# Channel words in half chunks, a fixed order for the last expert slots, and VectorE's part in the first mixing batch

## The chip, the cores and the metric

The kernel runs on one core of a Trainium2 chip. The metric is the device time of one execution in microseconds (us). The engines are TensorE (PE in the profile, with PEld for its weight loads), VectorE (DVE), ScalarE (ACT), GpSimd (POOL) and SyncE (SP, which issues nearly all DMAs).

## What is computed

Three stages follow each other: attention, a mixture of experts, and a mixing layer. The first two only set the stage here; of the third the reference says, for x of shape (4, 576, 512):

```
theta = x @ w_theta
zr, zi = x * cos(theta), x * sin(theta)
y = einsum('ts,bsd->btd', w_tok_r, zr) + einsum('ts,bsd->btd', w_tok_i, zi)
u = x + y
out = u + maximum(u @ w_ch, 0)
```

The experts give each token `p[e] * (relu(x @ w1[e]) @ w2[e])` for the one expert e that its gate chooses. The weights of the mixing layer come as 64-bit floating-point numbers.

## The kernel before

Products are made from high and low parts: an operand is rounded to fp32r by a ScalarE copy (the high part), a subtraction gives what is left (the low part), and three matmuls stand for one. So a weight or an activation needs a copy on ScalarE and a subtraction on VectorE or GpSimd before TensorE can take it.

**Experts.** Tokens are sorted by expert into slots: three early single slots, one late single slot, eight slots of two blocks of 128 tokens, and two final single slots, 14 in all, numbered by `i` in `run_slots`. `two_step` does a slot of two blocks, `single_step` one of 128 tokens. A step loads the next slot's weights (`load_w1`, `load_w2`), splits them (`split_w1`, `split_w2`, L1097 and L1098), gathers and transposes its tokens (`tokens`, L939), runs the hidden layer (`hidden`, L1024 to L1030), and finishes the slot before (`finish_slot`, L1063 to L1067). The finished rows are scaled on ScalarE (L1080) and scattered to memory by GpSimd (L1086). The scaled rows of a slot of two blocks and the relu of a single slot (L1037) share one buffer, `h`. The steps `i` up to `n + 1` also finish what is left over.

**Decoding.** The 64-bit mixing weights are read as pairs of 32-bit words and turned into fp32 on the way, in the idle time of the slots. `stage_words` asks for a chunk (L1153), and `decode_chunk` is a generator of four VectorE steps (L1189, L1193, L1196, L1198), with a square on GpSimd (L1190); `split_last` then gives the high part on ScalarE (L1179) and the low part on GpSimd (L1180). `decode(k)` advances it by k steps. The channel weights `w_ch` are the last, from slot `CHANNEL_AT` = 11 on: four chunks of 512 columns, with one buffer for words and one for values.

**Order.** PE, ACT and DVE follow the order of the program inside a `manual_schedule` block; SP and POOL are ordered by the scheduler of the compiler. Each slot is a block of its own, and the instructions of neighbouring blocks can be put among each other.

**Mixing.** Tokens are handled in four batches, each in two halves of 256 columns (`dh`). `theta` makes the angle in three groups of token chunks (two of 512 columns, the third of 256), `wave_steps` turns a group into zr and zi in steps, each `yield` ending one: range reduction on VectorE (L1398 to L1404), sine and cosine on ScalarE (L1405 to L1407), products with x on VectorE (L1410, L1412, L1419), then the high parts on ScalarE (L1426) and the low parts on GpSimd (L1427). `wave("0011")` advances groups 0, 0, 1, 1 by one step each. `mix` adds up 27 matmuls in the order of `MIX_ORDER` (L1440 to L1442), `mix_out` adds x (L1453) and, behind every second mix, splits the sum (L1455, L1456). There are two buffers for the result of a mix. `channel` is the last product, `store` the output. The calls in `mix_all` are the order of PE, ACT and DVE.

Of the kernel before, what the change touches and what calls it, by code (L numbers as in the profile page):

```python
# [10 lines left out]
F32 = mybir.dt.float32  # L11
# [3 lines left out]
AF = mybir.ActivationFunctionType  # L15
# [6 lines left out]
DM = H * D  # L22
# [13 lines left out]
WARM = 10  # L36
RING, HIDDEN_STEPS, LAST_STEPS = 3, 4, 5
MANUAL = {mybir.EngineType.PE, mybir.EngineType.Activation, mybir.EngineType.DVE}
# [14 lines left out]
class Kernel:  # L53
    def __init__(self, ctx, tc, ins, out, scratch):
        self.ctx, self.tc, self.nc = ctx, tc, tc.nc
        self.ins, self.out = ins, out
        self.scratch = scratch
        self.dec = iter(())

# [3 lines left out]
    def constants(self):  # L63
# [11 lines left out]
        scr = cp.tile([P, 256], I32, name="scr_i")  # L75
        self.w8 = cp.tile([P, E], F32, name="w8")
        nc.gpsimd.iota(scr[:, 0:E], pattern=[[-1, E]], base=E, channel_multiplier=0)
        nc.gpsimd.tensor_copy(self.w8, scr[:, 0:E])
        self.ebase = cp.tile([P, E], F32, name="ebase")
        nc.gpsimd.iota(scr[:, 8:8 + E], pattern=[[NT, E]], base=0, channel_multiplier=0)  # L80
# [698 lines left out]
    def run_slots(self, state, first=True):  # L779
# [10 lines left out]
        for i in range(0 if first else -1, n + 2):  # L790
            if first and i == OPEN_AT:
                self.right.close()
                self.open_mix_weights()
            if first and i == CHANNEL_AT:
                self.open_channel_weights()
            with self.tc.manual_schedule(engines=MANUAL):
                self.slot_step(state, i, first)

    def slot_step(self, state, i, first=True):
# [20 lines left out]
    def two_step(self, now, nxt, last, old, after):  # L820
# [4 lines left out]
        for f in range(4):  # L825
# [13 lines left out]
            elif f < 3:  # L839
                self.split_w2(now, f)  # L840
            self.decode(STEPS[0])
        for c in range(3):
# [9 lines left out]
        for c in range(2, 4):  # L852
            self.split_w1(nxt, c)
        self.decode(STEPS[1])
        for h in range(2):
# [3 lines left out]
    def single_step(self, now, nxt, last, old, final, over, begin, after):  # L859
# [6 lines left out]
        if final:  # L866
            self.decode(HIDDEN_STEPS)
        if nxt:
            for c in range(2):
                self.load_w1(nxt, c)  # L870
                self.split_w1(nxt, c)
        if now:
            self.relu(now, 0)
        if nxt:
            for c in range(2, 4):
                self.load_w1(nxt, c)
                self.split_w1(nxt, c)
        if now:
            self.relu(now, 1)
# [224 lines left out]
    def open_mix_weights(self):  # L1104
# [13 lines left out]
        self.todo += [(self.wt[:, 0, i], self.wt[:, 1, i], rows[j]) for i, j in enumerate(MIX_ORDER)]  # L1118
        self.active, self.last, self.one_val = [], [], False
        self.dec = self.decoder()  # L1120
# [3 lines left out]
    def open_channel_weights(self):  # L1124
# [4 lines left out]
            [P, 2, 4, DM], F32R, name="ch")  # L1129
        self.open_stage(1, 1)  # L1130
        self.one_val = True
        self.todo = self.square_words("moe2_w_ch", self.ch)
        self.stage_words()

# [47 lines left out]
    def decode_chunk(self, h, l, w, last):  # L1182
        nc = self.nc
        lo, hi = w[:, :, 0], w[:, :, 1]
        if self.one_val:
            self.split_last(last)
        val = self.val.tile([P, h.shape[1]], F32, name="val")
# [11 lines left out]
        last.append((h, l, val))  # L1199
        self.stage_words()  # L1200
        yield 1
# [26 lines left out]
    def mix_all(self):  # L1228
# [16 lines left out]
        self.prep(0, (), (3, 4))  # L1245
        self.wave("0000" "21111" "00" "0" "2222" "11" "1" "22" "2")
        self.waves(0, 1)
        self.wave("012")
        self.rest = []
        for b in range(B):  # L1250
            more = b + 1 < B
            self.mix(b, 0, 0)
            while self.rest:
                self.rest.pop(0)()
            self.mix_out(b, 0, 0)
            self.wave("0011" "0" if b else "01010101")
            self.mix(b, 0, 1)
            self.mix_out(b, 0, 1)
            self.wave("1" if b else "2222" "0011" "01")
            self.mix(b, 0, 2)  # L1260
            self.mix_out(b, 0, 2)
            self.wave("222")
            self.mix(b, 0, 3)
            self.mix_out(b, 0, 3)
            if more:
                self.load_x(b + 1)
# [4 lines left out]
            self.mix(b, 1, 1)  # L1271
            self.mix_out(b, 1, 1)
            if more:
                chunks = (2, 3) if b % 2 == 0 else (2, 3, 4)
# [11 lines left out]
            self.mix(b, 1, 3)  # L1286
            self.mix_out(b, 1, 3)
            if more:
                self.theta(b + 1, 1, 0)
# [91 lines left out]
    def wave_steps(self, b, dh, g):  # L1381
# [39 lines left out]
        else:  # L1421
            r = x
        for z, n in ((k, "r"), (q, "i")) if g < 2 else ((r, "m"),):
            zh = self.zp.tile([P, w, HD], F32R, name=f"z{n}h{g}")
            zl = self.zp.tile([P, w, HD], F32R, name=f"z{n}l{g}")
            nc.scalar.activation(zh, z, AF.Copy)  # L1426
            nc.gpsimd.tensor_tensor(zl, z, zh.bitcast(F32), ALU.subtract)  # L1427
            for i, c in enumerate(cs):
                st["z", dh, 8 if n == "m" else c + 4 * (n == "i")] = zh[:, i], zl[:, i]

    def mix(self, b, dh, g):
# [12 lines left out]
    def mix_out(self, b, dh, g):  # L1444
# [8 lines left out]
        nc.vector.tensor_tensor(u[:, zs], st["y"], st["xf", dh][:, d, zs], ALU.add)  # L1453
        if z == 1:
            nc.scalar.activation(uu[:, 0], u, AF.Copy)  # L1455
            nc.vector.tensor_tensor(uu[:, 1], u, uu[:, 0].bitcast(F32), ALU.subtract)  # L1456

# [101 lines left out]
```

## Time and profile before

| | us |
|---|---|
| median of 3 runs | 854.56 (854.49 to 854.65) |
| the profiled execution | 854.62 |
| its span, first to last instruction | 852.8 |
| TensorE busy | 811.4 (95%) |
| VectorE busy | 609.9 (72%) |
| ScalarE busy | 493.9 (58%) |
| GpSimd busy | 210.9 (25%) |

The profile covers the span; 1.82 us of the execution's time lie outside it. A busy share is an average over stages with different limits. Experts end and mixing begins at about 604 us.

### The profile page before, as it was taken

Reading aid. Unit: us, or ns where it says so; the run is one execution under the profiler, and the core shown is the slowest. Engines: PE = TensorE matmul, PEld = TensorE weight load, DVE = VectorE, ACT = ScalarE, POOL = GpSimd, SP = SyncE. Lnnn points to the kernel's source line nnn. Section 1 sums busy time; section 2 is a strip of 40 time slices with the busy share of each in tenths; the row PEclk is TensorE's granted clock in tenths of the full one; section 3 lists DMA queues with packets and bytes.
Section 4 is the critical chain, followed back from the end, with each engine's and each line's share of the span. In section 5 each row is a group of like instructions: output and inputs, shape, how many; then the busy total and the mean of one; then the engine's idle time right before and its main releaser. Section 6 shows DMA issues by size and latency. Waiting matters only on the chain.

```text
span 852.8 us, 15168 instructions
## 1 busy us (share of the span) xinstructions
PE 811.4 (95%) x5554; PEld 651.8 (76%) x5554; DVE 609.9 (72%) x1281; ACT 493.9 (58%) x883; POOL 210.9 (25%) x209
## 2 busy tenths in 40 slices
PE   7999999999999987899999999997898999999997
PEld 5555556656566555578999889985788999999997
DVE  6888787888979848856878888777486635755422
ACT  5888776777776654655665555546554435435311
POOL 3000002002103014421645554532023320332120
PEclk9999999999999999899999999999999999999999
DMA  6522323222430279226887778576101030020101
GB/s 162 157 70 61 100 59 94 84 64 58 114 102 26 60 257 241 62 69 211 294 290 267 268 247 275 180 286 215 51 1 51 13 106 2 13 93 1 57 1 56
DMA packets 65577, 102.68 MB, mean 120 GB/s; under 512 B 28242, under 2 KB 34774, under 8 KB 65496
## 3 DMA queue, kind: packets, MB, share of 16 engines
q1 hardware_dynamic: 61304, 91.13, 34.6%
q0 software_dynamic: 4192, 10.51, 3.6%
q8 instruction: 46, 0.75, 0.4%
q14 instruction: 35, 0.29, 0.1%
HBM read 98.67 MB, written 16.58 MB: 135 GB/s over the span
## 4 chain that ended last, share of the span: by engine, by line
PE 67%; DVE 14%; DMA 8%; issue 6%; ACT 3%; POOL 2%; another core or an unknown queue 0%; SPq 0%; POOLq 0%; DVEq 0%; ACTq 0%
PE o L402 7%; PE s L289 7%; PE t L361 5%; PE y L1442 4%; PE y L1440 4%; PE y L1441 4%; DVE ns L309 2%; PE v L1467 2%; PE o L398 2%; PE v L1468 2%; PE v L1466 2%; DVE stk L1098 2%; DVE a L347 2%; PE h L997 2%; PE h L996 2%
## 5 line engine op out<-in xcount | busy, mean ns | idle before, releaser
L315 ACT ACTIVATE e<-ns,nb 128x576 f32<-128x576 f32 x144 | 111.8, 777 | 44.9 <-DVE ns L309 43.1
L309 DVE TENSOR_SCALAR_CACHE_REDUCE ns<-s,nqs 128x576 f32<-128x576 f32 x144 | 116.6, 810 | 27.1 <-PE s L289 15.8
L347 DVE SCALAR_TENSOR_TENSOR a<-ns,thr,e 128x576 f32<-128x576 f32 x144 | 117.0, 813 | 1.5 <-ACT thr L322 1.1
L289 PE MATMUL s<-raw 64*128 64x288 f32 x512 | 87.6, 442 | 7.8 <-DVE ns L309 7.4
L362 ACT ACTIVATE aT<-t 128x512 f32<-128x512 f32 x128 | 70.3, 593 | 21.5 <-PE t L361 19.5
L402 PE MATMUL o<-aT,vm 128*64 128x288 f32 x512 | 76.3, 418 | 0.0
L995 PE MATMUL h<-xh,stk 128*128 128x256 f32 x256 | 73.2, 286 | 0.0
L996 PE MATMUL h<-xl,stk 128*128 128x256 f32 x256 | 72.5, 283 | 0.0
L997 PE MATMUL h<-xh,stk 128*128 128x256 f32 x256 | 72.4, 283 | 0.0
L361 PE MATMUL t<-ident,a 128*128 128x128 f32 x512 | 69.5, 276 | 1.5 <-ACT aT L362 1.5
L1098 DVE TENSOR_TENSOR w2l<-w2r,w2h 128x1024 fp32r<-128x1024 f32 x50 | 64.9, 1306 | 7.8 <-ACT w2h L1097 6.5
L289 PEld LDWEIGHTS s<-raw 64*128 64x128 f32 x512 | 42.3, 186 | 36.3 <-DVE ns L309 17.1
L361 PEld LDWEIGHTS t<-ident,a 128*128 128x128 f32 x512 | 57.0, 142 | 14.2 <-issue 10.1
L402 PEld LDWEIGHTS o<-aT,vm 128*64 128x64 f32 x512 | 31.5, 136 | 37.1 <-issue 23.8
L1097 ACT ACTIVATE w2h<-w2r 128x1024 fp32r<-128x1024 f32 x50 | 52.3, 1058 | 10.8 <-DMA w2r<-in_moe_w_dram 7.2
L1013 PE MATMUL o<-w2l,hh 128*128 128x512 f32 x128 | 50.1, 392 | 0.5 <-DVE w2l L1098 0.4
L1012 PE MATMUL o<-w2h,hh 128*128 128x512 f32 x128 | 50.6, 395 | 0.0
L1427 POOL TENSOR_TENSOR zrl<-tk,zrh 128x512 fp32r<-128x512 f32 x16 | 24.9, 1557 | 102.3 <-ACT zrh L1426 101.7
L1014 PE MATMUL o<-w2h,hl 128*128 128x512 f32 x128 | 49.9, 390 | 0.0
L995 PEld LDWEIGHTS h<-xh,stk 128*128 128x128 f32 x256 | 49.1, 192 | 0.8 <-DVE hl L1000 0.3
L996 PEld LDWEIGHTS h<-xl,stk 128*128 128x128 f32 x256 | 49.1, 192 | 0.5 <-issue 0.2
L997 PEld LDWEIGHTS h<-xh,stk 128*128 128x128 f32 x256 | 49.1, 192 | 0.0
(382 smaller groups left out, 2163.1 us busy)
## 6 DMA issues: line engine op xcount, KB each, us to landing
w2r<-in_moe_w_dram SPq DMA_DIRECT2D x56, 512.0 KB
raw<-in_moe_w_dram SPq DMA_DIRECT2D x42, 512.0 KB
raw<-in_q_dram SPq DMA_DIRECT2D x15, 576.0 KB
w1r<-in_moe_w_dram SPq DMA_DIRECT2D x14, 512.0 KB
raw<-in_k_dram SPq DMA_DIRECT2D x30, 176.0 KB
vm<-in_v_dram SPq DMA_DIRECT2D x32, 128.0 KB
scr_x<-x SPq DMA_DIRECT2D x16, 256.0 KB
out_dram<-ob SPq DMA_DIRECT2D x16, 256.0 KB
```

Of the source, the lines that this page charges most:

```text
L289: nc.tensor.matmul(s[:, z, :SH], qd[rows, int(j != z), cs], kd[rows, j * KH:j * KH + SH], start=True, stop=True)
L309: nc.vector.tensor_scalar(ns, s[:, :, :SH], self.nqs[:, 0:1], None, ALU.mult, ALU.min, accum_out=nb)
L315: self.nc.scalar.activation(e, pr["s", c, j], AF.Exp, bias=pr["nb", c][:, j:j + 1], scale=-1.0)
L347: nc.vector.scalar_tensor_tensor(a.rearrange("p (z s) -> p z s", z=2), s, thr, e, ALU.is_le, ALU.mult, accum_out=total)
L361: nc.tensor.transpose(t[:, i, :], al(c)[:, k * P:(k + 1) * P], self.ident)
L362: nc.scalar.activation(aT[:, 4 * j:4 * j + 4, c * P:(c + 1) * P], t, AF.Copy)
L402: nc.tensor.matmul(o[j * D:(j + 1) * D, :SH], vm[:, j, c - 1, :], aT[:, 4 * j + c - 1, zs], start=(z == 0 and c == 1), stop=(z == 1 and c ...
L995: nc.tensor.matmul(h[:, i], wh[:, fs], xh, start=(k == 0), stop=False)
L996: nc.tensor.matmul(h[:, i], wh[:, fs], xl, start=False, stop=False)
L997: nc.tensor.matmul(h[:, i], wl[:, fs], xh, start=False, stop=(k == 3))
L1097: nc.scalar.activation(hi, raw, AF.Copy)
L1098: nc.vector.tensor_tensor(lo, raw, hi.bitcast(F32), ALU.subtract)
```

## The change

It has three parts. The channel words are read in eight half chunks of 256 columns, with two buffers for words and three for values; they are asked for at set places (`more_words`), two at a time, and no longer at the end of a chunk. The decode counts are doubled. The slots 11 to 15 stand in one `manual_schedule` block. In the first mixing batch VectorE makes the low parts, one step after the copies; the order of waves is another, and the split of a sum is a function of its own, `mix_split`, called for the first batch behind its last mix of the half. Two constant tiles move to another pool.

```diff
-RING, HIDDEN_STEPS, LAST_STEPS = 3, 4, 5
+RING, HIDDEN_STEPS, LAST_STEPS = 3, 8, 10
...
+            if first and i >= CHANNEL_AT:
+                break
             with self.tc.manual_schedule(engines=MANUAL):
                 self.slot_step(state, i, first)
+        if first:
+            with self.tc.manual_schedule(engines=MANUAL):
+                for i in range(CHANNEL_AT, n + 2):
+                    self.slot_step(state, i, first)
...
-            self.decode(STEPS[0])
+            self.decode(STEPS[0] << self.halves)
+        self.more_words()
         for c in range(3):
             self.load_w2(nxt, c)
...
-        self.decode(STEPS[1])
+        self.decode(STEPS[1] << self.halves)
...
         if final:
             self.decode(HIDDEN_STEPS)
+            self.more_words()
...
             for c in range(2, 4):
                 self.load_w1(nxt, c)
                 self.split_w1(nxt, c)
+                if c == 2:
+                    self.more_words()
...
-        self.open_stage(1, 1)
-        self.one_val = True
-        self.todo = self.square_words("moe2_w_ch", self.ch)
-        self.stage_words()
+        self.open_stage(2, 3)
+        self.halves, n = True, DM // 2
+        w = self.words("moe2_w_ch")
+        self.todo = [
+            (self.ch[:, 0, k, z:z + n], self.ch[:, 1, k, z:z + n], [(slice(0, P), w[k * P:(k + 1) * P, z:z + n])])
+            for k in range(4) for z in (0, n)]
+        self.more_words()
+
+    def more_words(self):
+
+        if self.halves:
+            for _ in range(2):
+                self.stage_words()
...
-        self.stage_words()
+        if not self.halves:
+            self.stage_words()
...
-        self.wave("0000" "21111" "00" "0" "2222" "11" "1" "22" "2")
+        self.wave("0000" "21111" "00" "0" "2222" "11" "0" "1" "2" "1" "2" "2" "2")
...
+            if b == 0:
+                self.wave("01")
             self.mix_out(b, 0, 0)
-            self.wave("0011" "0" if b else "01010101")
+            self.wave("0011" "0" if b else "010101" "2222")
             self.mix(b, 0, 1)
             self.mix_out(b, 0, 1)
-            self.wave("1" if b else "2222" "0011" "01")
+            if b:
+                self.mix_split(b, 0)
+            self.wave("1" if b else "00" "0" "11" "0" "1")
             self.mix(b, 0, 2)
             self.mix_out(b, 0, 2)
-            self.wave("222")
+            self.wave("222" if b else "212" "2")
             self.mix(b, 0, 3)
             self.mix_out(b, 0, 3)
+            if b == 0:
+                self.wave("2")
+                self.mix_split(b, 0)
+            self.mix_split(b, 1)
...
             nc.scalar.activation(zh, z, AF.Copy)
-            nc.gpsimd.tensor_tensor(zl, z, zh.bitcast(F32), ALU.subtract)
+            if b:
+                nc.gpsimd.tensor_tensor(zl, z, zh.bitcast(F32), ALU.subtract)
...
+        if b == 0:
+
+            yield
+            for z, zh, zl in parts:
+                nc.vector.tensor_tensor(zl, z, zh.bitcast(F32), ALU.subtract)
...
-        if z == 1:
-            nc.scalar.activation(uu[:, 0], u, AF.Copy)
-            nc.vector.tensor_tensor(uu[:, 1], u, uu[:, 0].bitcast(F32), ALU.subtract)
+
+    def mix_split(self, b, k):
+
+        nc = self.nc
+        u, uu = self.state3[b]["u", k]
+        nc.scalar.activation(uu[:, 0], u, AF.Copy)
+        nc.vector.tensor_tensor(uu[:, 1], u, uu[:, 0].bitcast(F32), ALU.subtract)
```

## Rows read from the trace of the kernel before

**Rows 1.** Waits of TensorE from 648 us on: total, times, longest.

```profile
PE v L1467 <- DVE uu L1456: 0.4, 1, 0.4
```

**Rows 2.** Stretches: length, busy time of PE, PEld, DVE, ACT, POOL, clock, DMA.

```profile
580.00:590.00 10.00, 8.84 (x32) 6.13 (x31) 8.63 (x11) 6.88 (x13) 2.86 (x2) 0.83 0.92 315
...
600.00:610.00 10.00, 6.97 (x42) 5.10 (x41) 2.19 (x5) 3.59 (x9) 0.97 (x1) 1.00 0.13 39
```

**Rows 3.** Timeline of TensorE, last slots: start, duration, instruction, [wait before, releaser].

```profile
570.46 0.39 PE L1024 MATMUL h<-stk,xh 128*128 128x512 f32 x1
...
574.54 1.88 PE L1030 MATMUL h<-raw,xf 128*128 128x512 f32 x4
...
579.62 0.66 PE L1050 MATMUL t<-ident,h 128*128 128x128 f32 x4 [2.76 <-ACT h L1037]
581.43 0.63 PE L1024 MATMUL h<-stk,xh 128*128 128x512 f32 x1 [1.16 <-ACT xh L942]
...
587.75 1.88 PE L1030 MATMUL h<-raw,xf 128*128 128x512 f32 x4
```

**Rows 4.** Timeline of ScalarE, last slots.

```profile
571.11 0.63 ACT L1179 ACTIVATE ch<-val 128x512 fp32r<-128x512 f32 x1 [6.08 <-DVE val L1198]
571.65 1.25 ACT L1080 ACTIVATE h<-o,idx 128x512 f32<-128x512 f32 x2
...
578.96 0.60 ACT L1037 ACTIVATE h<-h 128x512 f32<-128x512 f32 x1 [1.61 <-DMA scr_m<-h,idx]
```

**Rows 5.** Timeline of GpSimd, last slots.

```profile
571.82 1.29 POOL L1180 TENSOR_TENSOR ch<-val,ch 128x512 fp32r<-128x512 f32 x1 [3.44 <-ACT ch L1179]
...
574.64 1.16 POOL L1086 DMA_INDIRECT scr_m<-h,idx  x1 [0.30 <-issue]
```

**Rows 6.** Timeline of VectorE, last slots.

```profile
568.40 0.43 DVE L1189 TENSOR_SCALAR val<-w 128x512 int32<-128x512 int32 x1 [2.18 <-POOL ch L1180]
...
575.59 2.38 DVE L1098 TENSOR_TENSOR stk<-w1r,stk 128x1024 fp32r<-128x1024 f32 x1
...
581.68 0.55 DVE L945 TENSOR_TENSOR xl<-t,xh 128x384 fp32r<-128x384 f32 x1
```

**Rows 7.** Timeline of SyncE's DMA issues, last slots.

```profile
559.89 0.35 SPq L1153 DMA_DIRECT2D w<-in_moe_w_ch_dram  x1
...
570.36 0.35 SPq L1153 DMA_DIRECT2D w<-in_moe_w_ch_dram  x1
```

**Rows 8.** Timeline of TensorE, first mixing batch.

```profile
622.86 0.30 PE L1440 MATMUL y<-wt,zrh 128*128 128x288 f32 x1
...
628.49 0.29 PE L1440 MATMUL y<-wt,zrh 128*128 128x288 f32 x1
...
632.05 0.30 PE L1440 MATMUL y<-wt,zrh 128*128 128x288 f32 x1
...
641.81 0.37 PE L1440 MATMUL y<-wt,zrh 128*128 128x288 f32 x1 [2.45 <-DVE u L1453]
...
647.92 1.03 PE L1356 MATMUL v<-ident,raw 128*128 128x128 f32 x8
```

**Rows 9.** Timeline of VectorE, first mixing batch.

```profile
618.72 0.68 DVE L1412 TENSOR_TENSOR tq<-tq,raw 128x512 f32<-128x512 f32 x1
619.33 0.28 DVE L1398 TENSOR_SCALAR tk<-tk 128x256 f32<-128x256 f32 x1
...
620.63 1.43 DVE L1404 TENSOR_SCALAR tr<-tr 128x256 f32<-128x256 f32 x1
621.99 1.79 DVE L1410 TENSOR_TENSOR tk<-tk,raw 128x512 f32<-128x512 f32 x1
```

**Rows 10.** Timeline of GpSimd, first mixing batch.

```profile
621.87 1.36 POOL L1427 TENSOR_TENSOR zil<-tq,zih 128x512 fp32r<-128x512 f32 x1
```

**Rows 11.** Timeline of ScalarE, first mixing batch.

```profile
632.59 0.63 ACT L1405 ACTIVATE tk<-tr 128x512 f32<-128x512 f32 x1 [4.43 <-DVE tr L1404]
...
635.91 0.67 ACT L1455 ACTIVATE uu<-u 128x576 fp32r<-128x576 f32 x1
```

More of the change, by code (lines that the diff above doesn't have):

```diff
@@ L57, in __init__ @@
         self.scratch = scratch
-        self.dec = iter(())
+        self.dec, self.halves = iter(()), False
     def chunk(self, c):
@@ L75, in constants @@
         scr = cp.tile([P, 256], I32, name="scr_i")
-        self.w8 = cp.tile([P, E], F32, name="w8")
+        self.w8 = self.rp.tile([P, E], F32, name="w8", bufs=1)
         nc.gpsimd.iota(scr[:, 0:E], pattern=[[-1, E]], base=E, channel_multiplier=0)
         nc.gpsimd.tensor_copy(self.w8, scr[:, 0:E])
-        self.ebase = cp.tile([P, E], F32, name="ebase")
+        self.ebase = self.rp.tile([P, E], F32, name="ebase", bufs=1)
         nc.gpsimd.iota(scr[:, 8:8 + E], pattern=[[NT, E]], base=0, channel_multiplier=0)
@@ L1118, in open_mix_weights @@
         self.todo += [(self.wt[:, 0, i], self.wt[:, 1, i], rows[j]) for i, j in enumerate(MIX_ORDER)]
-        self.active, self.last, self.one_val = [], [], False
+        self.active, self.last, self.halves = [], [], False
         self.dec = self.decoder()
@@ L1184, in decode_chunk @@
         lo, hi = w[:, :, 0], w[:, :, 1]
-        if self.one_val:
-            self.split_last(last)
         val = self.val.tile([P, h.shape[1]], F32, name="val")
@@ L1272, in mix_all @@
             self.mix_out(b, 1, 1)
+            self.mix_split(b, 2)
             if more:
@@ L1287, in mix_all @@
             self.mix_out(b, 1, 3)
+            self.mix_split(b, 3)
             if more:
@@ L1422, in wave_steps @@
             r = x
+        parts = []
         for z, n in ((k, "r"), (q, "i")) if g < 2 else ((r, "m"),):
@@ L1425, in wave_steps @@
             zl = self.zp.tile([P, w, HD], F32R, name=f"z{n}l{g}")
+            parts.append((z, zh, zl))
             nc.scalar.activation(zh, z, AF.Copy)
-            nc.gpsimd.tensor_tensor(zl, z, zh.bitcast(F32), ALU.subtract)
+            if b:
+                nc.gpsimd.tensor_tensor(zl, z, zh.bitcast(F32), ALU.subtract)
             for i, c in enumerate(cs):
                 st["z", dh, 8 if n == "m" else c + 4 * (n == "i")] = zh[:, i], zl[:, i]
+        if b == 0:
+            yield
+            for z, zh, zl in parts:
+                nc.vector.tensor_tensor(zl, z, zh.bitcast(F32), ALU.subtract)
     def mix(self, b, dh, g):
```

## The prediction

> **What bounds the kernel now.** I read the waits of TensorE first, then its granted clock by stretches, then the timelines of the engines around each wait. From 648 us to the end TensorE waits 0.4 us in all [rows 1]; that part is its own work, and whatever is won before 648 us reaches the end whole. So the question is what TensorE loses between the last expert slots (from 570 us) and 648 us. There are two places.
>
> The first is the tail of the experts. TensorE stands still for 2.76 us before 579.62 and 1.16 us before 581.43 [rows 3], and then runs part of the next stretch at the lower of its two clock levels: the mean granted clock of 580 to 590 us is 0.83 [rows 2], and the matmul at 581.43 took 0.63 us where the same line took 0.39 at 570.46 [rows 3]. What ends the first wait is ScalarE's relu at 578.96, which had waited for a scatter to land, because the relu writes the buffer that the scatter reads [rows 4]. The scatter was issued by GpSimd at 574.64, behind a channel-word subtraction at 571.82 that itself waited 3.44 us for ScalarE's copy [rows 5]; the copy at 571.11 waited 6.08 us for VectorE [rows 4]; VectorE's decode at 568.40 waited 2.18 us for GpSimd to give back the only value buffer [rows 6]. A serial chain of single buffers thus sits in front of a scatter.
>
> The second is the first batch of the mixing. A mix is 27 matmuls and takes 3.56 us where nothing is missing (628.49 to 632.05). The first one takes 5.63 us (622.86 to 628.49). The fifth starts at 641.81 after a wait of 2.45 us for a sum on VectorE, and the next work stands at 647.92, 6.1 us later [rows 8]. GpSimd's low parts come one after another at 1.36 us each [rows 10], and while they run VectorE is slowed: a 256-wide clamp took 1.43 us though the 256-wide subtraction at 619.33 took 0.28, and a 512-wide product took 1.79 us at 621.99, where one at 618.72 took 0.68 [rows 9, 10].
>
> **Words in half chunks.** The four chunks of 512 columns become eight of 256, each with the same four VectorE steps, one GpSimd square, one ScalarE copy and one GpSimd subtraction. No step falls away. A step of half the width costs a little over half: a 512-wide one starts the next 0.61 us later (618.72 to 619.33), and three 256-wide ones take 1.30 us (619.33 to 620.63 [rows 9]), 0.43 each. That is 0.13 us more than half, on 32 steps 4 us more of VectorE over 40 us; it lies in the time in which VectorE now waits (2.18 us before 568.40 alone [rows 6]) or TensorE's output matmuls run, and where that cover is gone it costs what is left of the 4 us. On SyncE's queue eight loads stand where four stood, of the same bytes.
>
> What changes is where a wait can sit. With two buffers, both halves of a chunk are asked for early, and three value buffers let VectorE start a half without waiting for GpSimd. The ScalarE copies that stand ahead of the last two-block slot's scaling are now those of the first pair of halves, finished in the hidden loop; they wait for nothing. Their pair of scalings then follows TensorE: its last output matmul before 570.46 ends at about 570.85 at the latest (0.39 us long [rows 3]), and the pair took 1.25 us for two [rows 4], so the second ends by 571.5 and its scatter is issued at 571.6 instead of 574.64. From issue to relu the scatter took 4.32 us (574.64 to 578.96 [rows 4, 5]); the relu comes at 575.9, 3.0 us earlier. The hidden layer itself frees the relu at about that time (its last four matmuls start at 574.54 [rows 3]), so more is not to be had there. The condition is that words three and four have landed by about 566 us. In the run before, the second whole chunk was asked for at 559.89 [rows 7], and VectorE came to it at 568.40, held by the value buffer and not by the load [rows 6]. I take landing in time.
>
> The third chunk was asked for at 570.36, waiting on VectorE, and stood ahead of the next slot's weight loads on the same queue [rows 7]. With words queued behind weights, this in-order wait is gone; its worth lies inside the 3.0 us.
>
> **Fixed order of the last slots.** Before, TensorE could take the next slot's first matmuls at 581.43 ahead of four of the old slot's transposes. In one order the transposes come first. They wait for a transpose bank that VectorE's subtraction at 581.68 frees (0.55 us long, ending 582.23, 3.27 us after the relu's start [rows 4, 6]). So the hidden layer starts at 575.9 + 3.3 + 0.5 for four transposes = 579.7 to 579.8, against 581.43: 1.6 us of the 3.0 remain. Its 18 split matmuls then take 4.08 us, as from 570.46 to 574.54, against 6.32 us before (581.43 to 587.75 [rows 3]), in which the four transposes and the slow clock lay: 2.2 us. The tail gives 1.6 + 2.2 = **3.8 us**. Bounds: nothing, if words land late; 6 us, if TensorE never waits (2.76 + 1.16 and about 1.8 of slow clock and transposes). VectorE's eight decode steps of the slot after stand between the old slot's subtractions and splits that wait for TensorE anyway; cover gone, they cost 3 us.
>
> On the clock: TensorE will still pause, some 1.6 us between the two groups of transposes. Row by row, the pause of 2.76 us was followed by the 0.83; the stretch 600 to 610 us, with TensorE busy for 6.97 of 10 us, kept 1.00 [rows 2, 3]. I take the full clock. The Trainium skill, "TensorE: Matmul & The Clock Gate", section "HAM oscillation — how this bites in real kernels", says that matmuls after a wait for data can start throttled, each time anew. The rows of this kernel show it after one pause and not after another; by that rule the hidden layer would stay at half speed and the sum would be 1.8 us less.
>
> **VectorE takes the low parts.** Ten subtractions move from GpSimd to VectorE, eight of 512 and two of 256 columns. The 512-wide product with two SBUF inputs starts the next instruction 0.61 us later [rows 9]; that is my price, 0.36 for 256: 5.6 us more on VectorE over 28 us. GpSimd's work leaves the stretch, and with it the slowing.
>
> First half: VectorE reaches the third group's steps at 619.33 as before. Four steps take 1.5 us (1.30 from 619.33 to 620.63, and 0.28 for the last [rows 9]), the second group's two products 1.2: 622.1. Then the first group's two low parts to 623.3, two half-tile products (0.36 each) to 624.0, the second group's low parts to 625.3, two products to 626.0, and the last low part about 626.7. TensorE asks for the first at 622.86 + 0.27, for the second group's 1.6 us later, for the last at about 626.1, so it loses some 0.7 us and ends at 627.1 instead of 628.49: **1.4 us**.
>
> Second half: VectorE has its first two subtractions, then the sum of mix one, by 628.4. Six 512-wide steps (0.61, the two clamps about 0.35) take 3.1 us, to 631.5; four 256-wide ones 1.5, to 632.9; the sum of mix two, 288 wide, 0.4, to 633.3. ScalarE needs 3.32 us for six activations (632.59 to 635.91 [rows 11]) from 631.2, so to 634.6, one more us for the third group, then the copies, about 0.6 us each (0.67 for 576 columns [rows 11]), from 635.6. VectorE multiplies until 635.9, subtracts the first group to 637.5 and gives the sum of mix three by 637.9. TensorE ends mix four at 627.1 + 3 x 3.56 = 637.8, so that sum, which cost 2.45 us before, is now just in time. The second group's low parts follow to 639.8, the last to 641.4 behind the sum of mix four; mix five needs them at 639.4, 640.2 and 641.1. It ends at about 641.6, against 648.1: with the 1.4 us, **6.5 us**. Bounds: 7.2 us at the most (1.4 + 0.7 + 2.45 + 2.6 over five mixes of 3.56), and 4 if each step is 0.1 us dearer, since the sums stand in one row with 25 others. The two splits of sums that are put behind cost VectorE and ScalarE 1.4 us each, after mix five's needs; the channel stage reads them only behind mix eight, and the three mixes of 3.56 us between cover them.
>
> **Sum.** Against the profiled execution's own span of 852.8 us, which stood in a time of 854.62 (1.82 us outside the span; the median of the runs is 854.56): 852.8 - 3.8 - 6.5 + 1.8 = 844.3 us.
>
> **Rivals.** One: SyncE's queue isn't among the three engines whose order is fixed, so words can still be asked for late; then VectorE and GpSimd wait as before and the tail gives nothing: 854.6 - 6.5 = 848.1. For it: the load at 570.36 came late in the run before. Against it: two buffers. Two: the hidden layer after the pause runs at the low clock: 846.1. Three: VectorE becomes the bound of the first batch, and only half the 6.5 us comes: 847.5. Four: TensorE doesn't pause at all in the tail: 842. Five: neither part acts, since waits only move to the next in line: 854.6. Six, slower: eight decode steps now stand in fixed order ahead of the next slot's weight splits, which began at 575.59 on VectorE [rows 6]. If words landed at 572.5 the tail would give nothing; later than 579 the loss eats the mixing's 6.5 us too; at 582 the time is 857.6. Against it: no load of words here was that late.
>
> **Numbers.** Forecast 0.55 (own range 842.3 to 846); late words 0.14; low clock 0.11; VectorE the bound 0.06; no pause 0.04; nothing 0.04; slower 0.06. Faster (by over 0.2%, 1.7 us, about what a measurement of this kernel can tell) 0.90, same 0.04, slower 0.06. The range 841.5 to 849.5 leaves out the last two, and takes in the low bounds.
>
> **What would show it.** Right: the scatter of the last two-block slot issued near 571.6; the relu at 576 ending no DMA wait; granted clock 1.00 in the hidden layer after it; VectorE's low parts at 0.68 us; no clamp above 0.5; TensorE's mixes one to five without a wait above 0.7 us. Wrong: a wait of VectorE or GpSimd for channel words, a wait of TensorE for a sum at mix five, or waits beyond 648 us less TensorE's gain.

## The result, and the profile after

| | before | after |
|---|---|---|
| median of 4 runs, us | 854.61 (854.49 to 854.80) | 847.92 (846.58 to 848.61) |
| ratio, 95% interval | | 0.992 (0.9902 to 0.9937) |
| profiled execution, its span, us | 854.62, 852.8 | 847.86, 846.1 |

Faster, by 6.7 us where 10.3 were forecast. Lines of the kernel after stand some ten to forty lines further down than before (relu L1047, scaling L1090, scatter L1096, low parts L1465).

**The mixing** did what the sum said. Timeline of TensorE, the starts of mix one, of mix two, and of what stands behind mix five:

```profile
622.17 0.29 PE L1476 MATMUL y<-wt,zrh 128*128 128x288 f32 x1
...
626.30 0.30 PE L1476 MATMUL y<-wt,zrh 128*128 128x288 f32 x1
...
640.70 1.03 PE L1384 MATMUL v<-ident,raw 128*128 128x128 f32 x8
```

Mix one takes 4.13 us in place of 5.63 [rows 8], a gain of 1.50 where 1.4 was forecast. The other four take 14.40 us in place of 19.43 (628.49 to 647.92), 5.03 where 5.1 was forecast, and there is no wait between them. On VectorE a product, a low part and the sum that used to stop mix five:

```profile
620.06 0.69 DVE L1438 TENSOR_TENSOR tk<-tk,raw 128x512 f32<-128x512 f32 x1
...
621.26 0.69 DVE L1465 TENSOR_TENSOR zrl<-tk,zrh 128x512 fp32r<-128x512 f32 x1
...
636.00 0.45 DVE L1489 TENSOR_TENSOR u<-y,xTf 128x288 f32<-128x288 f32 x1
```

The 512-wide low part takes 0.69 us, and the next instruction starts 0.61 us behind it (621.87), as priced; GpSimd took 1.36 [rows 10]. The 512-wide product that took 1.79 us beside GpSimd's low parts [rows 9] takes 0.69; GpSimd does nothing between 613 and 640 us. The sum of mix three starts at 636.00; mix five, which needs its buffer, starts at 637.10 without a wait.

**The tail of the experts** did not. Timeline of TensorE, from the first matmul of slot 12's hidden layer to the last four of slot 13's:

```profile
567.27 0.39 PE L1034 MATMUL h<-stk,xh 128*128 128x512 f32 x1
...
571.36 1.88 PE L1040 MATMUL h<-raw,xf 128*128 128x512 f32 x4
...
575.67 0.66 PE L1060 MATMUL t<-ident,h 128*128 128x128 f32 x4 [2.00 <-ACT h L1047]
578.34 1.11 PE L1060 MATMUL t<-ident,h 128*128 128x128 f32 x4 [2.02 <-DVE xl L955]
579.11 0.78 PE L1034 MATMUL h<-stk,xh 128*128 128x512 f32 x1
...
584.37 1.88 PE L1040 MATMUL h<-raw,xf 128*128 128x512 f32 x4
```

This stretch takes 17.10 us, and 17.29 before (570.46 to 587.75 [rows 3]): 0.19 us less, where 3.8 was forecast. The two waits, 4.0 us in all, are no shorter than the 2.76 and 1.16 of before. Timelines of SyncE's issues, GpSimd and ScalarE in order of time show why:

```profile
563.35 0.34 SPq L972 DMA_DIRECT2D w1r<-in_moe_w_dram  x1
563.99 1.03 SPq L972 DMA_DIRECT2D raw<-in_moe_w_dram  x2
...
566.84 0.84 SPq L1172 DMA_DIRECT2D w<-in_moe_w_ch_dram  x2
...
568.63 0.99 POOL L1096 DMA_INDIRECT scr_m<-h,idx  x1 [0.30 <-issue]
...
575.02 0.60 ACT L1047 ACTIVATE h<-h 128x512 f32<-128x512 f32 x1 [3.76 <-DMA scr_m<-h,idx]
```

The scatter is issued 1.36 us behind the hidden layer's first matmul, as forecast (1.1), where it was 4.18 before (570.46 to 574.64 [rows 3, 5]). But the relu that waits for it comes 6.39 us behind the issue, where it was 4.32 [rows 4, 5]. The loads of weights and words, which moved forward too, stand ahead of it. The stretches of the same time (length, busy time of PE, PEld, DVE, ACT and POOL, each with its count of instructions, clock, DMA share, GB/s):

```profile
568.00:570.00 2.00, 2.00 (x11) 1.65 (x10) 0.07 (x1) 1.23 (x2) 1.31 (x2) 1.00 1.04 330
570.00:572.00 2.00, 2.00 (x9) 1.50 (x8) 1.86 (x2) 1.06 (x1) 0.00 (x0) 1.00 0.93 273
572.00:574.00 2.00, 1.67 (x7) 0.69 (x5) 0.51 (x1) 0.00 (x0) 0.69 (x2) 1.00 0.59 237
574.00:576.00 2.00, 0.33 (x3) 0.33 (x4) 0.00 (x0) 0.98 (x2) 0.53 (x1) 1.00 0.02 6
...
578.00:580.00 2.00, 1.66 (x6) 1.56 (x7) 1.71 (x3) 2.00 (x3) 0.00 (x0) 0.50 0.81 247
580.00:582.00 2.00, 2.00 (x7) 1.52 (x7) 2.00 (x3) 2.00 (x6) 0.14 (x1) 0.65 0.93 330
```

The DMA engines are nearly full until about 573 and empty from 574, and at 575 the relu starts: by these rows the scatter lands as the last of all that was asked for. GpSimd also waited 3.43 us for words five (to 573.04), which I had set down as a sign of being wrong; nothing waited for what it then made. The granted clock is 0.50 and 0.65 behind the two waits: that is the rival of the low clock.

**Behind the experts** time was lost that no step of mine had. Timeline of TensorE, first before, then after: the last output matmuls, the token transposes, the first theta matmul.

```profile
601.21 1.88 PE L1067 MATMUL o<-w2r,hf 128*128 128x512 f32 x4
604.24 0.77 PE L1356 MATMUL v<-ident,raw 128*128 128x128 f32 x5 [1.15 <-ACTq L764]
606.84 1.36 PE L1356 MATMUL v<-ident,raw 128*128 128x128 f32 x11 [1.83 <-issue]
607.95 0.36 PE L1377 MATMUL th<-th,xTh 128*128 128x256 f32 x1
```

```profile
597.85 1.88 PE L1077 MATMUL o<-w2r,hf 128*128 128x512 f32 x4
603.12 3.68 PE L1384 MATMUL v<-ident,raw 128*128 128x128 f32 x16 [3.39 <-ACTq L764]
606.45 0.56 PE L1405 MATMUL th<-th,xTh 128*128 128x256 f32 x1
```

From the end of the output matmuls to theta it is 4.86 us before and 6.72 after. The 16 transposes take 2.13 us before and 3.68 after, at half the clock, and theta goes on at it for a while: from theta to mix one it is 14.91 us before and 15.72 after. A stretch of after, with the clock at 0.50 (in before it is 1.00 from 602 to 610 us):

```profile
604.00:606.00 2.00, 2.00 (x12) 2.00 (x11) 0.94 (x2) 1.21 (x3) 0.00 (x0) 0.50 0.13 47
```

The bill of the two profiles: 3.19 us gained up to slot 12's first matmul (570.46 to 567.27), 0.19 in the tail, 0.02 lost in the output matmuls, 1.86 lost to theta, 0.81 lost to mix one, 6.53 in the five mixes, 0.52 lost behind them: 6.7. The first is no part of the sum; the runs below say what it is.

### The profile page after: what moved, and what is told of

The parts are those of the page before. It is cut to its first block, busy times and chain, and to the rows that moved or that the text cites. A ratio compares the mean times of both kernels' runs of the same rounds, so it can differ in the third digit from the quotient of the medians.

```text
span 846.1 us, 15208 instructions
## 1 busy us (share of the span) xinstructions
PE 811.0 (96%) x5554; PEld 654.4 (77%) x5554; DVE 610.4 (72%) x1307; ACT 495.0 (59%) x887; POOL 200.5 (24%) x207
## 5 line engine op out<-in xcount | busy, mean ns | idle before, releaser
L289 PEld LDWEIGHTS s<-raw 64*128 64x128 f32 x512 | 42.1, 186 | 36.4 <-DVE ns L309 17.3
L361 PEld LDWEIGHTS t<-ident,a 128*128 128x128 f32 x512 | 56.9, 141 | 14.3 <-issue 10.1
L1108 DVE TENSOR_TENSOR stk<-raw,stk 128x1024 fp32r<-128x1024 f32 x36 | 44.6, 1261 | 8.1 <-ACT stk L1107 8.0
```

What stands on the lines that cost most here:

```text
L289: nc.tensor.matmul(s[:, z, :SH], qd[rows, int(j != z), cs], kd[rows, j * KH:j * KH + SH], start=True, stop=True)
L361: nc.tensor.transpose(t[:, i, :], al(c)[:, k * P:(k + 1) * P], self.ident)
L1108: nc.vector.tensor_tensor(lo, raw, hi.bitcast(F32), ALU.subtract)
```

## The experiments

My theory: the mixing part gives all of the gain; the tail part gives nothing, since the relu shares the scatter's buffer and the scatter now lands behind more transfers; and the loss behind the experts belongs to the change, through the last decode. Rivals: the tail works and is lost again behind the experts; the loss there has nothing to do with the change. Four stretches of each profile, from rows of TensorE's timeline as above: **tail**, slot 12's first hidden matmul to slot 13's last four; **branch**, end of the last output matmul to the first theta matmul, and in it the busy time of the 16 **transposes**; **theta**, from there to mix one; **mixes**, one to five. All in us, the stretches from one execution each; the ratio is to the kernel before on the same chip, with its 95% interval. Executions of one kernel differ by more than the result's table shows: 31 runs of before beside the first four experiments took 851.92 to 859.73 us, median 855.48.

| run | tail | branch | transposes | theta | mixes | median | ratio, interval |
|---|---|---|---|---|---|---|---|
| before | 17.29 | 4.86 | 2.13 | 14.91 | 25.06 | 854.61 | |
| after | 17.10 | 6.72 | 3.68 | 15.72 | 18.53 | 847.92 | 0.992 (0.9902 to 0.9937) |
| e1_mix | 18.28 | 4.69 | 2.13 | 14.86 | 18.52 | 848.37 | 0.9929 (0.9909 to 0.995) |
| e2_tail | 18.59 | 6.30 | 3.34 | 15.09 | 24.99 | 855.48 | 1.0002 (0.998 to 1.0025) |
| e3_consts | 19.40 | 5.70 | 3.28 | 16.42 | 24.98 | 856.01 | 1.0004 (0.9984 to 1.0023) |
| e4_order | 18.63 | 6.16 | 3.24 | 16.46 | 25.37 | 855.63 | 0.9998 (0.9973 to 1.0022) |
| e5_own | 13.08 | 6.71 | 3.57 | 14.72 | 18.51 | 843.32 | 0.988 (0.9855 to 0.9905) |
| e6_late | 16.74 | 6.76 | 3.60 | 14.86 | 18.53 | 848.25 | 0.9934 (0.9911 to 0.9957) |
| e9_dve | 18.23 | 6.65 | 3.51 | 14.73 | 18.52 | 848.49 | 0.9933 (0.991 to 0.9955) |
| e10_both | 14.51 | 5.17 | 1.97 | 14.89 | 18.53 | 842.5 | 0.9869 (0.9846 to 0.9892) |
| e12_before_own | 16.59 | 5.44 | 3.28 | 15.11 | 24.90 | 852.83 | 0.9991 (0.9969 to 1.0012) |
| e13_xlate | 14.52 | 6.22 | 3.20 | 15.22 | 18.51 | 844.68 | 0.9895 (0.9868 to 0.9922) |
| e14_nowords | 15.66 | 6.74 | 3.57 | 14.72 | 18.51 | 846.68 (one run) | |
| e15_dummy | 15.11 | 7.12 | 1.97 | 15.35 | 18.52 | 847.21 | 0.993 (0.9902 to 0.9959) |

**One part at a time.** e1_mix is before with the mixing functions of after; e2_tail is after with the mixing functions of before.

> Only the mixing part: VectorE takes the low parts of the first batch, new order of waves, splits put behind. Theory A (the mixing part is worth what the trace after shows between the first mix and the first transposes of the next batch, some 5.5 us, and nothing is given back later): 849 us if the 3.2 us that the changed kernel has ahead of the eleventh slot are not in this part, 846 if they are. Theory B (the mixing part only wins because the tail of the experts is over earlier): 852 or more.

> Only the tail part: half chunks, two word buffers, fixed order, moved constants; mixing as before. Theory A (tail gains 0.2 us up to the last output matmul and loses some 2.3 us behind it, since GpSimd passes the branch late): 856.5 us, or 853.5 if the 3.2 us ahead of slot eleven come with it. Theory B (the tail was worth 3.8 us and the loss behind it belongs to the mixing part): 851 us or less.

e3_consts moves only the two constant tiles:

```diff
-        self.w8 = cp.tile([P, E], F32, name="w8")
+        self.w8 = self.rp.tile([P, E], F32, name="w8", bufs=1)
...
-        self.ebase = cp.tile([P, E], F32, name="ebase")
+        self.ebase = self.rp.tile([P, E], F32, name="ebase", bufs=1)
```

e4_order only puts slots 11 to 15 in one block:

```diff
+            if first and i >= CHANNEL_AT:
+                break
...
+        if first:
+            with self.tc.manual_schedule(engines=MANUAL):
+                for i in range(CHANNEL_AT, n + 2):
+                    self.slot_step(state, i, first)
```

> Only the two constant tiles in the other pool. Theory A (the 3.2 us ahead of slot eleven come from how the whole program is laid out, not from these tiles): 854.6 us, within 0.3. Theory B (they come from where these and the later tiles lie): 851.4 us, with VectorE's wait of 1.8 us near 139 us gone.

> Only the slots from eleven on in one fixed order; words stay in whole chunks with single buffers. Theory A (order alone keeps the serial chain ahead of the scatter, and puts the last decode steps behind the last subtractions, with GpSimd late at the branch): slower, 856 to 859 us. Theory B (order alone is what shortens the hidden layer's stretch by 2 us): 852.5 us.

The mixing part alone takes 7.1 us off the median; everything else together takes nothing, and neither do the two pieces of it that were run alone (the half chunks alone were not run). e4_order came neither slower nor faster, so neither of its theories holds. That the mixing gains by VectorE's low parts and not by the new order of waves is not separated: e1_mix has both. The mixes take 18.51 to 18.53 us in all nine profiles that have that part, and 24.90 to 25.37 in the five that do not. Slot 12 begins at 567.0 to 569.8 us in all other profiles, of either kind, and at 570.46 only in that of before (means of 569.0 with whole chunks, 568.2 with half chunks): by these means most of the 3.19 us ahead of it is what one execution differs from another.

**The shared buffer.** e5_own is after, with slot 11's scaled rows in memory that nobody else uses then:

```diff
+        if self.halves:
+            self.gather(after)
+            self.spare = after["xt"][:, 1]
...
-            if h == 0:
-                st["obs"] = self.hg.tile([P, F], F32, name="h")
-            ob, o = st["obs"][:, h * DM:(h + 1) * DM], st["o"][h]
+            if self.halves:
+                ob, o = (self.raw[:, 3 * F:3 * F + DM] if h else self.spare), st["o"][h]
...
```

> The kernel after, but the scaled rows of slot 11 stand in memory of their own and no longer in the buffer of the next slot's relu. Theory (the scatter's landing, 6.4 us after its issue, holds the relu): the relu follows the hidden layer's last four matmuls within 1.5 us and ends no wait for a transfer; from the first matmul of slot 12's hidden layer to the last four of slot 13's it takes 13 to 14.5 us in place of 17.1, and the time is 2.5 to 4 us below that of the kernel after, ratio to before 0.988 to 0.99. Rival (VectorE's weight split is next in line, 0.5 us behind): the stretch takes 16 to 16.7 us. Rival (the buffer does not matter): 17.1 us and ratio 0.992.

Timelines of ScalarE and TensorE in e5_own, and a stretch behind the pause:

```profile
573.65 0.60 ACT L1050 ACTIVATE h<-h 128x512 f32<-128x512 f32 x1 [1.16 <-PE h L1043]
...
576.97 0.65 PE L1063 MATMUL t<-ident,h 128*128 128x128 f32 x4 [1.63 <-DVE xl L958]
```

```profile
578.00:580.00 2.00, 2.00 (x10) 1.62 (x9) 2.00 (x3) 2.00 (x6) 0.00 (x0) 1.00 0.93 272
```

The relu now waits for TensorE's own matmuls, and of the two pauses one of 1.63 us is left, with the clock at 1.00 behind it (576 to 582 us). The tail takes 13.08 us, where my step had 13.4 (9.3 to slot 13's first hidden matmul and 4.08), and it is reached by an edit that the change lacks. The median is 843.32 us; on the same chip e6_late and e9_dve below, which leave the shared buffer, have 848.25 and 848.49. e12_before_own makes the same edit in the kernel before:

> The kernel before, with nothing changed but the memory of slot 11's scaled rows, which is their own as in the run with that edit on the kernel after. If the shared buffer alone held the tail, the stretch from slot 12's hidden layer to slot 13's last four matmuls falls to 13 to 14.5 us, as there, and the time is 3 to 5 us below before (ratio near 0.995). Rival: the whole-chunk words in front of the weight loads on SyncE's queue hold the weight copies that stand ahead of the relu on ScalarE; then the relu comes 1 to 2 us earlier at the most, the stretch is 16 to 17.5 us (17.3 to 19.4 in the three profiles of this tail so far), and the half chunks are needed as well.

Timelines of SyncE, ScalarE, VectorE and TensorE in e12_before_own:

```profile
568.80 0.35 SPq L1159 DMA_DIRECT2D w<-in_moe_w_ch_dram  x1
569.47 1.02 SPq L965 DMA_DIRECT2D raw<-in_moe_w_dram  x2
...
573.90 1.06 ACT L1103 ACTIVATE stk<-raw 128x1024 fp32r<-128x1024 f32 x1 [1.62 <-DMA raw<-in_moe_w_dram]
574.86 0.58 ACT L1040 ACTIVATE h<-h 128x512 f32<-128x512 f32 x1
...
572.19 0.43 DVE L1195 TENSOR_SCALAR val<-w 128x512 int32<-128x512 int32 x1 [2.73 <-DMA w<-in_moe_w_ch_dram]
...
579.76 1.11 PE L1053 MATMUL t<-ident,h 128*128 128x128 f32 x4 [1.36 <-DVE xl L948]
```

The rival's stretch came, 16.59 us, and no gain in the median, but its cause is the smaller part. With whole chunks the words are asked for late and ahead of the weights, and the weight copy that stands ahead of the relu waits for them; yet the relu starts 5.96 us behind slot 12's first matmul, only 0.8 us later than in e5_own (5.14), and 2.5 us earlier than in before (8.50), where the rival had 2 at the most. Most of the difference of 3.5 us lies behind the relu: VectorE waits 2.73 us for the words of a decode whose steps stand ahead of its weight splits and among them, its low part `xl` starts 10.26 us into the stretch in place of 7.86, TensorE waits for it, and the clock falls to 0.50 (580 to 582 us). So the tail needs both, memory of its own for the rows and the change's tail part; either alone gives nothing that the median shows. Whether the half chunks or the fixed order are what it needs of the change is not separated.

**Why the scatter lands late.** e6_late moves the request for words five and six behind `load_w2(nxt)`:

```diff
-                if c == 2:
-                    self.more_words()
...
             for c in range(3):
                 self.load_w2(nxt, c)
+            self.more_words()
```

> The kernel after, but words five and six are asked for behind slot 13's second weights and no longer ahead of slot 11's second scatter. Theory (the two loads of words ahead of the scatter delay its landing): the relu starts 4.3 to 5.2 us after the scatter's issue in place of 6.4, and the stretch from slot 12's hidden layer to slot 13's last four matmuls is 15.5 to 16.3 us in place of 17.1. Rival (the three weight loads of 512 KB set the landing, words or not): 6.2 to 6.6 us and 17.1 us. In both the words come later, and if that counts, the decode of the last slots ends later and the time rises by up to 2 us.

Timelines of SyncE and GpSimd in e6_late:

```profile
567.81 0.84 SPq L1171 DMA_DIRECT2D w<-in_moe_w_ch_dram  x2
...
569.60 0.99 POOL L1095 DMA_INDIRECT scr_m<-h,idx  x1 [0.30 <-ACT h L1089]
```

SyncE still asks 1.8 us ahead of the scatter, as in after: its order is the compiler's, and the edit did not reach it. The run says nothing on the words; its relu comes 6.01 us behind the issue. e14_nowords takes the loads away:

```diff
...
-                if c == 2:
-                    self.more_words()
+                if c == 2 and self.halves and self.todo:
+                    for k in range(2):
+                        h, l, _ = self.todo.pop(0)
+                        self.staged.append((h, l, self.kept[k + 2]))
...
```

> The kernel after, but the loads of the fifth and sixth half chunk, 0.5 MB asked for just ahead of the scatter, are left out, and the third and fourth are decoded again in their place. If the scatter lands when the bytes asked for ahead of it have passed at about 300 GB/s, 0.5 MB less brings the relu from 6.0 to 6.8 us behind the issue to 4.3 to 5.1, and the stretch to 15.4 to 16.6 us. If the scatter has its own time, the words change nothing: 6.0 to 6.8 us and 16.7 to 18.2 us.

Timelines of GpSimd and ScalarE in e14_nowords:

```profile
569.99 0.99 POOL L1098 DMA_INDIRECT scr_m<-h,idx  x1 [0.33 <-ACT h L1092]
...
574.94 0.60 ACT L1049 ACTIVATE h<-h 128x512 f32<-128x512 f32 x1 [2.14 <-DMA scr_m<-h,idx]
```

The relu comes 4.95 us behind the issue, where the four profiles with these loads and the shared buffer have 6.01, 6.39, 6.67 (e2_tail) and 6.77 (569.58 to 576.35 in e9_dve); the tail falls to 15.66. Against these four, half a megabyte less brings the landing 1.1 to 1.8 us forward, and 0.5 MB at some 300 GB/s is 1.7. But the kernels with memory of their own show the landing too, by the loads of the mixing's first tokens, which wait for it (575.14 in after, 0.12 us behind the relu). From the scatter's issue to these loads it is 5.51 us in e5_own, up to 6.94 in the other seven with the words, and 5.11 here. So the words' share is between 0.4 and 1.8 us, from one execution: it points to the bytes ahead of the scatter and does not settle it.

**Behind the experts.** e9_dve gives the last two low parts to VectorE; e10_both has this and the edit of e5_own.

```diff
-            nc.gpsimd.tensor_tensor(l, val, h.bitcast(F32), ALU.subtract)
+            eng = nc.vector if self.halves and not self.active else nc.gpsimd
+            eng.tensor_tensor(l, val, h.bitcast(F32), ALU.subtract)
```

> The kernel after, but the low parts of the last two half chunks are made by VectorE and not by GpSimd. Theory (GpSimd comes last to the branch behind the experts, held by these two low parts): GpSimd passes it before 599 us, the last scatter is issued within 0.5 us of ScalarE's last scaling, and from the last output matmul to the first theta matmul it takes 4.9 to 5.4 us in place of 6.7. The clock: full in the first theta matmuls if the pause is near 1.5 us, which gives 0.8 us more. Rival (ScalarE, behind the same copies, comes last): 6.3 to 6.8 us, no change of the time.

> Both of these in one: slot 11's scaled rows in memory of their own, and the last two low parts on VectorE. If the two losses are separate, the gains add up: 13 to 14.5 us in the tail's stretch, 4.9 to 5.4 us behind the experts, and a time 4 to 6 us below that of the kernel after, near 842 to 844 us. Rival (what is won in the tail is waited for at the end, since the last words land late): the stretch behind the experts grows by what the tail gives, and the time is that of the kernel after.

Timelines of GpSimd and TensorE in e9_dve, and of TensorE in e10_both:

```profile
603.07 0.99 POOL L1096 DMA_INDIRECT scr_m<-raw,idx  x1 [5.06 <-ACT raw L1090]
...
605.41 3.51 PE L1385 MATMUL v<-ident,raw 128*128 128x128 f32 x16 [3.39 <-ACTq L764]
```

```profile
600.40 1.97 PE L1391 MATMUL v<-ident,raw 128*128 128x128 f32 x16 [3.45 <-ACTq L764]
```

The theory falls here. GpSimd is free, the last scatter follows the scaling (602.11 + 0.69) by 0.27 us, and TensorE waits 3.39 us all the same. In e10_both it waits 3.45 us, but the transposes behind it take 1.97 us and the branch 5.17: a clock that stays up is worth the 1.5 us, and the wait itself is not what GpSimd sets. The numbers expected of e10_both came (14.51, 5.17 and 842.5), but the 5.17 is luck: in e13_xlate below, which has the same two edits, the transposes take 3.20 us and the branch 6.22. e15_dummy, on top of e13_xlate, fills the pause with matmuls whose result nobody uses:

```diff
+        if not now and not last and old and old["final"]:
+            d = self.ps_h.tile([P, 2, 2 * P], F32, name="h").rearrange("p a b -> p (a b)")
+            for k in range(10):
+                nc_ = self.nc
+                nc_.tensor.matmul(d, old["xh"][:, 0, :P], self.stk[0][:, :512], start=True, stop=True)
```

> The run with the later token loads, and ten matmuls of 512 columns on old operands behind the last output matmul, 2.3 us of work that computes nothing that is used. If the pause behind the experts is what lets the clock fall, the transposes and the theta matmuls behind it run at full clock in every execution: the 16 transposes take about 2 us, and the first theta matmul starts no later than without. If TensorE's own way past the branch starts only after its last matmul, theta starts up to 2.3 us later and the time rises by as much.

Timelines of TensorE and ScalarE in e15_dummy, the last GpSimd row of the branch's line (instruction, its duration in ns, start), and a stretch in the tail:

```profile
602.31 1.97 PE L1395 MATMUL v<-ident,raw 128*128 128x128 f32 x16 [0.98 <-ACTq L764]
...
605.43 1.57 ACT L1396 ACTIVATE xTh<-v 128x512 fp32r<-128x512 f32 x3 [5.65 <-DMA scr_m<-raw,idx]
...
606.13 0.36 PE L1416 MATMUL th<-th,xTh 128*128 128x256 f32 x1 [1.86 <-ACT xTh L1396]
```

```profile
L764 POOLq INC_SWDGE_SEM  x1: 1500/1500/1500, 603.4 to 603.4; - x1
```

```profile
578.00:580.00 2.00, 2.00 (x8) 1.59 (x8) 2.00 (x3) 2.00 (x6) 0.00 (x0) 0.66 0.98 282
```

Both expectations came half true. The transposes run at full clock, 3.3 us behind the last real output matmul as without. But GpSimd passes the branch only at 603.4 to 604.9, ScalarE's first copy comes at 605.43, and theta starts later than ever, 7.12 us behind the output matmuls; that GpSimd's late pass is what holds the copy is not shown. The cover of the pause costs at least what the clock gives: branch and theta together take 22.47 us, and 21.44 in e13_xlate. The run also speaks on the tail: its relu is not late and it has one pause there, of 2.07 us, and the clock still falls to 0.66 and 0.50 behind it (578 to 582 us); the tail takes 15.11.

**A wait for weights.** In e10_both slot 13's last four matmuls wait 1.28 us for a weight load that stands behind loads of tokens on SyncE's queue. e13_xlate is e10_both, and asks for those tokens a step later:

```diff
...
         if over:
+            self.load_first_x()
             self.decode(LAST_STEPS)
...
-        if final:
-            self.load_first_x()
...
```

> Own memory for slot 11's rows and the last two low parts on VectorE, and the loads of the mixing's first tokens asked for one step later, behind slot 13's last weight load and not ahead of it. If those loads, which wait for slot 11's scatter to land, hold the weight load behind them on SyncE's queue, TensorE's wait of 1.28 us for weights at slot 13's last four matmuls goes, the stretch is 13 to 13.3 us and the time 841 to 842.5 us by the same ratio scale (0.985 to 0.987). If they do not, 14.5 us and 0.987. If the tokens then come late behind the experts, the time rises.

Timeline of SyncE, then of TensorE, in e13_xlate:

```profile
577.74 0.80 SPq L1379 DMA_DIRECT2D raw<-scr_m  x2
579.22 0.35 SPq L974 DMA_DIRECT2D raw<-in_moe_w_dram  x1
...
584.30 1.98 PE L1042 MATMUL h<-raw,xf 128*128 128x512 f32 x4 [1.27 <-DMA raw<-in_moe_w_dram]
```

Again the compiler's order on SyncE is as it was, and so is the wait; whether the tokens' place costs it, this run does not say. e5_own speaks for it: in the same order, the scatter landed 1.3 us sooner there, the weight load went out 8.17 us into the stretch and not 9.47 as in e10_both, and there is no such wait. As far as these rows show, the kernel is thus e10_both a second time. The best versions are e10_both and e5_own: 0.987 and 0.988 where the change has 0.992. The intervals of e10_both and of the change are apart; those of e5_own and of e13_xlate, 0.9895, overlap with the change's. Between e5_own and e10_both no difference is shown.

## Why the prediction was right or wrong

The sum gave 844.3 us; 847.92 came. That is faster, as forecast, and inside the wide range of 841.5 to 849.5, but outside the forecast's own 842.3 to 846: one of the two terms held. In number it is rival one (848.1, the mixing without the tail), but not for that rival's reason: of the engines only GpSimd waited for words, and its wait held nothing up.

**First mixing batch, 6.5 us: right,** in size and in place: 6.53 in the profiles, 7.1 in the medians of e1_mix, 1.50 and 5.03 in its two halves against 1.4 and 5.1. The low part cost what the 512-wide product costs, the slowing of VectorE went with GpSimd's work (a 512-wide product 0.69 us in place of 1.79), and the sum that was to be just in time was.

**Tail, 3.8 us: wrong, and this is the step that failed:** "From issue to relu the scatter took 4.32 us". I carried that over to an earlier issue. The scatter did go out 2.8 us earlier in the stretch, but the loads had moved with it: 2 MB of weights and words are asked for in the 5.3 us ahead of it, where before it was 1.5 MB, on DMA engines that were busy for 0.34 of 570 to 572 us. The landing took 6.39 us in the profile of after, and 6.0 to 6.8 in the others with the shared buffer and these loads. In after that is 7.75 us from the hidden layer's first matmul to the relu, where I had 5.4 and before had 8.5. From the relu on, the steps to slot 13's first hidden matmul held within 0.3 us (4.1 us, forecast 3.9). Then the 18 split matmuls took 5.26 us instead of 4.08, which is rival two. Against the 13.4 us that these steps add up to, 3.7 are missing: 2.3 are the landing, 1.2 the clock and 0.2 the rest. That the bytes ahead set the landing is supported by e14_nowords and not settled; that the shared buffer turned it into a wait is shown by e5_own. The rival of the low clock did not need the late relu: the clock fell behind two pauses of 2 us in after, and behind one of 2.07 in e15_dummy, whose relu is on time; behind one of 1.63 in e5_own, e10_both and e13_xlate it held. The Trainium skill, "TensorE: Matmul & The Clock Gate", section "HAM oscillation — how this bites in real kernels", says that matmuls behind a wait for data can start throttled. The trace of after agrees (0.50 and 0.65), and I had set one row of before against it.

Over the profiles the tail is 17.3, 18.3 and 19.4 us in the three kernels with the old tail, and 16.7 to 18.6 in the four with the new one: means of 18.3 and 17.7. With memory of its own for slot 11's rows as well it is 13.1 to 15.1 in four, with a mean of 14.3.

**Full clock behind the experts: taken without a word.** I took theta as it was in the one profile of before. Its transposes ran at full clock there and in e1_mix, and at a lower one in the other three kernels with the old words; with the new words at a lower one in seven of eight (e15_dummy, with its unused matmuls, is not counted). From the last output matmul to mix one the old words take 20.9 us in the mean of five profiles, the new ones 21.4 in that of eight. So most of the 2.7 us lost between these two profiles is what one execution differs from another; about 0.5 us is left for the change, against 0.6 gained in the tail. That adds up to the ratio of 1.0002 of e2_tail, though each of these two means is uncertain by about as much as it says.

**Words in time, fixed order, decode's cover: right but worth nothing.** Words three and four were there, VectorE's decode held nothing up in after, and e4_order alone moves nothing. The rivals of late words and of a bound VectorE did not come.

## What to carry to other kernels

A transfer that took 4.32 us in one place took 6.0 to 6.8 behind more loads: when work on one queue is moved ahead, look at what then stands ahead of the transfer, and do not carry over its time from another place. If an engine waits for a scatter to land only because it writes the scatter's source next, give the source its own memory; in the tail that was worth more here than all the reordering, but only together with it. And take a stretch in which the clock falls now and then from several executions before a difference of 2 us in it is explained.

## What the hardware showed that I had not expected

Behind the experts stands a branch around slots that this input does not need. ScalarE's way past it, from its compare to its semaphore, by the rows of the branch's line in before and in after:

```profile
L764 ACTq COMPARE_BRANCH  x1: 50/50/50, 603.7 to 603.7; - x1
L764 ACTq EVENT_SEMAPHORE  x1: 17/17/17, 604.2 to 604.2; - x1
```

```profile
L764 ACTq COMPARE_BRANCH  x1: 50/50/50, 600.4 to 600.4; - x1
L764 ACTq EVENT_SEMAPHORE  x1: 17/17/17, 603.1 to 603.1; - x1
```

It takes 0.4 to 0.5 us in all five kernels with whole chunks of words and 2.6 to 2.8 in all nine with half chunks. TensorE's wait of 3.3 to 3.5 us ends with it (0.98 in e15_dummy, which fills it). In the kernels with whole chunks TensorE goes on after 1.15 to 1.29 us but then stands still for another 1.4 to 2.0 us with no releaser in the profile, 2.5 to 3.3 us in all, so that little is lost. What keeps ScalarE is open; no run here took it away.
